# Rebuilding the preparation of an attention training kernel: token-major projections, DMA transposes, compact 16-row transposes in DRAM and zero-padded head tiles

## The chip, the cores and the metric

The kernel runs on one core of one Trainium2 chip. The metric is device time of one launch in microseconds (us), lower is better. Engines are named as the profile names them: PE (TensorE matmuls), DVE (VectorE), ACT (ScalarE), POOL (GpSimd) and SP (SyncE, which here only issues DMAs; the profile writes SPq for its sequencer).

## The reference

A transformer block with conditioned layernorms, forward and backward in one launch. Its outputs are the block's output and nine gradients.

```python
x = A_x                                     # 1 x 2048 tokens x 512, bf16
mod = (silu(c) @ w_mod).reshape(1, 6, 1, 512)
sa, ca, ga, sb, cb, gb = mod[:, 0], ..., mod[:, 5]
h = layernorm(x) * (1 + ca) + sa            # "h1" below
q, k, v = split(h @ wqkv)                   # 32 heads of width 16
p = softmax(q @ k.T * 16 ** -0.5)
x = x + ga * ((p @ v) @ wo)
h = layernorm(x) * (1 + cb) + sb
x = x + gb * (relu(h @ w1 + b1) ** 2 @ w2 + b2)     # w1: 512 x 1792
# outputs: x, and the vjp of x for grad_out with respect to
# A_x, A_wqkv, A_wo, B_w1, B_b1, B_w2, B_b2, c, w_mod
```

The kernel replaces the row maximum of the softmax by a bound: minus the norm of q times the largest norm of k of that head ("m rows"). It rides in the score matmul as a 17th row next to the 16 rows of q.

## The kernel before: what the change and the argument touch

Scores are computed for four heads at once, each in 32 rows of a 128-row tile: 16 rows of data, one auxiliary row, 15 zero rows. `n` is 2048, `P` 128, `D` 512, `TT` 16, `HG` 8 (groups of four heads, called "heads" below when the backward loads them), `QC` 4.

Preparation: layernorm, transposes on PE, token-major q/k/v, then the projections once more, now with padded weights, to get q, k and v transposed and padded:

```python
    POOL.memset(vaug[:], 1.0)
    # ... (cut) wqkv_nat loaded
    POOL.memset(wpadT[:], 0.0)
    # ... (cut) wqkv_nat copied into wpadT in slots of 32 columns; wpad_st stored
    for t in range(TT):
        ln_stats(x0_tok[:, t, :], mean1, rstd1, t, wk)      # about ten small DVE operations
        # ... (cut) xn1, h1t by DVE, h1_st stored; xn1 transposed by PE into xn1T
    # ... (cut) sum over tokens of grad_out by 16 matmuls -> gradient of b2
    for t in range(TT):
        for which in range(3):
            # 4 matmuls into pq
            if which < 2:
                DVE.tensor_copy(qtmp[:, 0:D], pq[:])
                # ... squares and sums for the norms by DVE; q_st / k_st stored
            else:
                DVE.tensor_copy(vaug[:, t, 0:H, 0:DH], pq.rearrange("p (h d) -> p h d", d=DH))
    # ... (cut) norms -> mrows, with 16 PE transposes
    for which, dstt in ((0, QtP), (1, KtP), (2, VtP)):
        for hg in range(HG):
            for qc in range(QC):
                pp = psB.tile([P, 512], F32, name="ppad", tag="pqkv")
                for ic in range(DC):
                    PE.matmul(pp[:], wpadT[:, ic, which, hg, :], h1T[:, ic, qc * 512:(qc + 1) * 512], ...)
                # DVE writes pp to stagep (plus auxsel, a 1 in the auxiliary row, for k and v)
            # for q: 4 row loads of mrows into stagep
            SP.dma_start(out=dstt[hg], in_=stagep[:])
```

Weight gradients of the dense part are summed over four chunks of tokens in DRAM, by DMAs that accumulate. Each piece passes through a `dwp` tile:

```python
                part = wk.tile([P, 512], F32, name="dwp", tag="dwp", bufs=3)
                DVE.tensor_copy(part[:, 0:w], acc[:, 0:w])
                if c == 0:
                    POOL.dma_start(out=dw_st[i][:, 0:w], in_=part[:, 0:w])
                else:
                    POOL.dma_start(out=dw_st[i][:, 0:w], in_=part[:, 0:w], accum_op=ALU.add)
```

Backward attention works through 512 units (64 for each of 8 heads). Each unit has 4 score matmuls, 4 dP matmuls, exponentials on ACT, two products `dS_u` on DVE, and one DMA transpose `dsT` issued by SP:

```python
        def load_head(hg):
            for key, src in (("q", QtP), ("k", KtP), ("v", VtP), ("do", dOtP)):
                st[key] = strm.tile([P, n], BF, name=f"i{key}", tag=f"i{key}")
                SP.dma_start(out=st[key][:], in_=src[hg])
            ACT.dma_start(out=qs[:], in_=q_st[:, :, hg * 64:(hg + 1) * 64])
        def transpose_unit(u):
            SP.dma_start(out=dqt[u // 4][:, qi], in_=bst[u][1].rearrange("p h k -> p (h k)"), transpose=True)
        load_head(0)
        for j in range(16):
            SP.dma_start(out=wT_pad[:, j, :], in_=wpad_st[:, j * P:(j + 1) * P], transpose=True)
        # ... (cut) the loop over units; load_head(hg + 1) is called early in head hg
```

## Time and profile before

The median of three runs was 3228.29 us (3228.0 to 3232.57).

The program falls into five stages. Their limits are taken from named operations in the trace: the first and last softmax exponential of the forward pass (`ET`), the first and last `dS_u` of the backward pass, and the end.

| stage | us |
|---|---|
| preparation: start to first ET | 290.0 |
| forward attention, dense chunks woven in: first to last ET | 1095.3 |
| dense tail: last ET to first dS_u | 194.4 |
| backward attention: first to last dS_u | 1464.0 |
| final gradients: to the end of the span | 181.4 |

Busy time of each engine in those stretches, kernel before. Columns: start and end, then length, then busy us of PE, PEld, DVE, ACT and POOL with the number of instructions, the granted PE clock, the DMA share (the time of the packets over the span of 16 engines, so it can pass 1: 1.14 below) and GB/s.

```profile
core 0: us, PE busy (x) PEld busy (x) DVE busy (x) ACT busy (x) POOL busy (x), PEclk, DMA share, GB/s
0.00:290.00 290.00, 175.34 (x803) 71.60 (x804) 213.76 (x451) 8.44 (x22) 33.46 (x62) 0.84 0.32 113
290.00:1385.40 1095.40, 906.09 (x5270) 245.31 (x5269) 341.58 (x627) 958.08 (x1034) 220.72 (x247) 0.77 0.47 100
1385.40:1579.80 194.40, 109.56 (x439) 43.32 (x439) 100.66 (x201) 11.77 (x18) 43.62 (x45) 0.76 0.70 154
1579.80:3043.80 1464.00, 1241.82 (x10212) 342.20 (x10208) 1190.75 (x1025) 1117.25 (x2203) 143.47 (x104) 0.84 1.14 205
3043.80:3225.20 181.40, 149.25 (x802) 64.80 (x801) 98.09 (x177) 46.27 (x94) 44.92 (x34) 0.90 0.44 124
```

In the preparation DVE is busy 214 of 290 us and PE 175, one after the other; ACT does almost nothing (8 us) and the DMA engines are idle two thirds of the time (0.32). Nothing of forward attention overlaps it. That is what the change goes for. The backward stage is the opposite: DMA share 1.14, with DVE, PE and ACT each busy more than three quarters of the time.

The costliest groups of instructions of the preparation, kernel before. Columns: line, engine, operation, output<-inputs, shapes and count; then busy us and mean ns of one; then the engine's idle time just before them, with what ended it.

```profile
L270 PE MATMUL ppad<-xn1T,wpadT 128*128 128x512 bf16 x384 | 97.9, 403 | 20.9 <-DVE stagep L273 16.2 <-DVE stagep L275 4.0 <-DVE vaug L246 0.5
L234 PE MATMUL pqkv<-wqkv_nat,xn1T 128*128 128x512 bf16 x192 | 48.1, 389 | 17.2 <-DVE vaug L246 13.4 <-DVE qtmp L239 2.0 <-DVE xn1T L217 1.8
L275 DVE TENSOR_SCALAR stagep<-ppad,auxsel 128x512 bf16<-128x512 f32 x64 | 48.0, 751 | 18.0 <-PE ppad L270 10.3 <-DMA stagep<-mrows 4.3
...
L108 DVE CAST crows<-cbf 1x512 f32<-1x512 bf16 x1 | 17.7, 17691 | 0.6 <-DMA cbf<-in_c_dram 0.6
```

The padded projections (`ppad`) cost twice what the q/k/v projections (`pqkv`) cost, for the same numbers laid out differently. The last line is an oddity: one cast of 512 numbers took 17.7 us, while POOL ran two large memsets.

### The profile page before, as it was taken

The page shows a single profiled execution, that of the slowest core. Times are in us where ns is not written, and L with a number is a line of the kernel's source. Part 1 is how long each engine was busy: PE and PEld are TensorE (multiplying, and loading weights), DVE is VectorE, ACT ScalarE, POOL GpSimd, SP SyncE. Part 2 cuts the span into 40 slices and gives each one's busy share as a digit, 9 for nine tenths or more (in the row PEclk, how much of TensorE's full clock was granted, in tenths as well). Part 3 has the DMA queues.
Part 4 walks back from the last instruction along what each step waited for, and adds up shares of the span by engine and source line. Part 5 has one row for each costly group of instructions (what it writes and reads, how often), then busy time and mean ns, then how long its engine had stood idle before and what let it go on. Part 6 is the DMA issues. An engine that isn't in the chain of part 4 may idle for free.

```text
span 3225.2 us, 47200 instructions
## 1 busy us (share of the span) xinstructions
PE 2582.1 (80%) x17521; PEld 767.2 (24%) x17521; DVE 1944.8 (60%) x2480; ACT 2141.8 (66%) x3369; POOL 486.2 (15%) x490
## 2 busy tenths in 40 slices
PE   2778998787887779655588888888888888988888
PEld 1222111222222222212122222222222222222233
DVE  8943001344443244345478787878878787878773
ACT  0004999898988789620178777877778787878632
POOL 3000000123122213322101010010101010000131
PEclk7987555798799779877679787988888787889889
DMA  4125011428247833968699999999999999999951
GB/s 157 61 88 168 28 30 42 77 86 214 67 96 142 138 82 87 167 119 178 195 203 200 212 197 214 200 213 203 205 208 198 213 196 215 196 213 196 220 152 57
DMA packets 1401343, 494.52 MB, mean 153 GB/s; under 512 B 1324168, under 2 KB 1364876, under 8 KB 1400728
## 3 DMA queue, kind: packets, MB, share of 16 engines
q1 hardware_dynamic: 1372216, 464.23, 72.2%
q0 software_dynamic: 12384, 25.17, 4.4%
q10 hardware_dynamic: 16512, 2.10, 0.5%
q8 instruction: 138, 2.26, 0.3%
q14 instruction: 93, 0.76, 0.1%
HBM read 93.93 MB, written 76.70 MB: 53 GB/s over the span
## 4 chain that ended last, share of the span: by engine, by line
PE 36%; DMA 24%; ACT 17%; DVE 11%; issue 7%; SPq 4%; POOL 1%; DVEq 0%; ACTq 0%; POOLq 0%
DMA dsT<-dS_u 16%; ACT ET L580 11%; PE psS_u L739 7%; PE dqacc L794 5%; ACT E_u L741 5%; PE accVK L776 3%; PE ppad L270 3%; PE accVK L767 2%; PE psST L578 2%; PE psS_x L739 2%; DVE dS_u L753 2%; PE pm L417 2%; PE pm L499 1%; PE pm L437 1%; PE pwq L989 1%
## 5 line engine op out<-in xcount | busy, mean ns | idle before, releaser
L753 DVE TENSOR_TENSOR dS_u<-psD_u,E_u 128x1024 bf16<-128x1024 f32 x1024 | 1188.5, 1217 | 279.3 <-PE psD_u L751 180.7
L741 ACT ACTIVATE E_u<-psS_u 128x512 bf16<-128x512 f32 x1536 | 869.3, 636 | 297.8 <-PE psD_u L751 284.2
L580 ACT ACTIVATE ET<-psST 128x1024 bf16<-128x1024 f32 x1024 | 949.8, 1260 | 136.0 <-PE psST L578 134.7
L739 PE MATMUL psS_u<-ik,iq 32*128 32x512 bf16 x1536 | 522.3, 438 | 14.0 <-DMA ik<-KtP 4.8
L751 PE MATMUL psD_u<-iv,ido 32*128 32x512 bf16 x2048 | 452.0, 435 | 36.0 <-DVE dS_u L753 30.9
L578 PE MATMUL psST<-qt_sb,kt_sb 32*128 32x512 bf16 x2048 | 399.1, 478 | 66.5 <-ACT ET L580 31.2
L741 ACT ACTIVATE E_u<-psS_x 128x512 bf16<-128x512 f32 x512 | 335.7, 656 | 23.2 <-PE psD_u L751 21.8
L794 PE MATMUL dqacc<-dsT,KS_tok 128*32 128x512 bf16 x2048 | 213.8, 505 | 165.7 <-DMA dsT<-dS_u 150.1
L594 PE MATMUL oacc<-ET,vaug 128*32 128x512 bf16 x2048 | 253.7, 486 | 1.3 <-DVE ostage L598 1.3
L776 PE MATMUL accVK<-E_u,dOs_tok 128*16 128x512 bf16 x2048 | 227.2, 434 | 1.2 <-DMA dOs_tok<-dOs_st 1.2
L739 PE MATMUL psS_x<-ik,iq 32*128 32x512 bf16 x512 | 212.3, 415 | 0.4
L809 POOL TENSOR_TENSOR dQacc<-dQacc,dqtmp 128x512 f32<-128x512 f32 x64 | 81.0, 1266 | 856.9 <-ACT dqtmp L804 856.9
L739 PEld LDWEIGHTS <-iq 32*128 32x128 bf16 x2048 | 100.0, 93 | 367.4 <-issue 366.9
L751 PEld LDWEIGHTS <-ido 32*128 32x128 bf16 x2048 | 124.3, 93 | 244.0 <-issue 218.9
L598 DVE COPY ostage<-oacc 128x512 f32<-128x512 f32 x32 | 22.0, 686 | 264.4 <-PE oacc L594 264.4
L578 PEld LDWEIGHTS <-kt_sb 32*128 32x128 bf16 x2048 | 83.8, 95 | 404.4 <-issue 393.6
L347 DVE COPY dwp<-pm 128x512 f32<-128x512 f32 (+1 forms) x102 | 67.2, 659 | 172.3 <-PE pm L340 91.3
L340 PE MATMUL pm<-tk,h_c 128*128 128x512 bf16 (+1 forms) x256 | 70.8, 408 | 70.5 <-DVE dwp L347 57.5
L767 PE MATMUL accVK<-dS_u,qz_12963 128*32 128x512 bf16 x1024 | 114.3, 435 | 7.5 <-ACT vkb L779 6.8
L767 PE MATMUL accVK<-dS_u,qz_12962 128*32 128x512 bf16 x1024 | 111.2, 424 | 7.1 <-ACT vkb L779 5.9
L270 PE MATMUL ppad<-xn1T,wpadT 128*128 128x512 bf16 x384 | 97.9, 403 | 20.9 <-DVE stagep L273 16.2
L794 PEld LDWEIGHTS <-KS_tok 128*32 128x32 bf16 x2048 | 52.4, 106 | 225.6 <-issue 170.3
(657 smaller groups left out, 2415.5 us busy)
## 6 DMA issues: line engine op xcount, KB each, us to landing
dw_st<-dwp POOLq DMA_DIRECT2D x90, 256.0 KB, 5.0
kt_sb<-KtP SPq DMA_DIRECT2D x32, 512.0 KB, 4.5
dsT<-dS_u SPq DMA_TRANSPOSE x512, 4.8
dwp<-dw_st SPq DMA_DIRECT2D x30, 256.0 KB, 5.0
wA<-in_B_w_dram SPq DMA_DIRECT2D x4, 1792.0 KB
wB<-in_B_w_dram SPq DMA_DIRECT2D x4, 1792.0 KB
QtP<-stagep SPq DMA_DIRECT2D x8, 512.0 KB, 2.9
KtP<-stagep SPq DMA_DIRECT2D x8, 512.0 KB, 2.6
```

The lines of the kernel that those rows point to most:

```text
L270: PE.matmul(pp[:], wpadT[:, ic, which, hg, :], h1T[:, ic, qc * 512:(qc + 1) * 512], start=(ic == 0), stop=(ic == DC - 1))
L578: PE.matmul(ps[:, hi, :], kt_sb[r:r + 32, kt * P:(kt + 1) * P], qt_sb[r:r + 32, :], start=True, stop=True, tile_position=(r, 0))
L580: ACT.activation(ET[:, 2 * pair:2 * pair + 2, :], ps[:], AF.Exp, scale=SCALE)
L594: PE.matmul(oacc[32 * hq:32 * hq + 32, :], lhsT, ET[:, hq, :], start=(kt == 0), stop=(kt == TT - 1), tile_position=(0, 32 * hq), skip_grou ...
L739: PE.matmul(psS[:], st["q"][r:r + 32, qt * P:(qt + 1) * P], st["k"][r:r + 32, kc * 512:kc * 512 + 512], start=True, stop=True, tile_positi ...
L741: ACT.activation(bst[u][0][:, hq, :], psS[:], AF.Exp, scale=SCALE)
L751: PE.matmul(psD[:, hi, :], st["do"][r:r + 32, qt * P:(qt + 1) * P], st["v"][r:r + 32, kc * 512:kc * 512 + 512], start=True, stop=True, til ...
L753: DVE.tensor_tensor(dS_u[:, 2 * pair:2 * pair + 2, :], psD[:], E_u[:, 2 * pair:2 * pair + 2, :], ALU.mult)
L767: PE.matmul(cur["vk"][32 * hq:32 * hq + 32, :], hst[hg]["qz"][:, qt, hq, :], bst[u][1][:, hq, :], start=(qt == 0), stop=False, tile_positi ...
L776: PE.matmul(acc[32 * hq:32 * hq + DH, :], dOs_tok[:, qt, (hg * 4 + hq) * DH:(hg * 4 + hq + 1) * DH], E_u[:, hq, :], start=False, stop=(qt ...
L794: PE.matmul(acc[32 * hq:32 * hq + 32, :], KS_tok[:, kc * 4 + kt, h * DH:h * DH + 32], tT[:, :, hq * 4 + kt, :], start=(kt == 0), stop=(kt ...
L809: POOL.tensor_tensor(dst2, dst, tmp[:], ALU.add)
```

## The change

The intent is to compute q, k and v once, token-major, to let the DMA engines transpose them, to keep the transposes compact in DRAM (16 rows for each head, no padding), and to load those rows into tiles whose padding was written once. Norms come from PE, with a selector matrix. Evictions are shared with ACT. In return every head tile is loaded in pieces of 16 rows (and one row). The padded weights for the last stage are built and transposed during forward attention instead of at the start of the backward. h1 is not stored but computed again in the last stage, and two buffers of `dwp` instead of three make room.

The core of the diff (cuts marked):

```diff
+    def load_rows(dst, srcT, hg, cols, aux=None):
+        for h in range(4):
+            i = hg * 4 + h
+            SP.dma_start(out=dst[32 * h:32 * h + DH, :], in_=srcT[i * DH:(i + 1) * DH, cols])
+            if aux is not None:
+                SP.dma_start(out=dst[32 * h + DH:32 * h + DH + 1, :], in_=aux[i:i + 1, cols])
# ... preparation (cut)
+        def layernorm(g):                    # groups of four token tiles, bn_stats/bn_aggr, xn1 by ACT
+                if ti % 2 == 1:
+                    SP.dma_start(out=h1T[:, t - 1:t + 1].rearrange(...), in_=h1_g[...], transpose=True)
+        def qkv(g):
+                for which in (1, 0, 2):      # 4 matmuls each
+                    if which == 0:
+                        DVE.tensor_copy(dst, pq[:])
+                    else:
+                        ACT.activation(dst, pq[:], AF.Identity)
+                SP.dma_start(out=qkT[:, :, t * P:(t + 1) * P], in_=qkv_g[:, ti, 0:2 * D], transpose=True)
+            SP.dma_start(out=qkT_st..., in_=qkT[:, :, cols])       # and v_st, k_st, q_st
+        def norms(g):
+            DVE.tensor_tensor(sq[:], qkT[:, :, cols], qkT[:, :, cols], ALU.mult)
+            # 8 matmuls with sel into pn[0:H]
-        for hg in range(HG):                 # the 384 padded projections, QtP, KtP, VtP (cut)
# ... forward attention (cut)
-        racc = ffw.tile([P, 4, D], F32, name="racc")
+        racc = ffw.tile([P, 5, D], F32, name="racc")   # 5th row: sum of grad_out, formerly by PE in preparation
-                part = wk.tile([P, 512], F32, name="dwp", tag="dwp", bufs=3)
+                part = wk.tile([P, 512], F32, name="dwp", tag="dwp", bufs=2)
-            SP.dma_start(out=kt_sb[:], in_=KtP[hg])
+            load_rows(kt_sb, qkT_st[1], hg, slice(0, n))
+        def later_stage(i):                  # 16 steps: v transposed, padded weights built and transposed to wT_st
# ... backward (cut)
-                SP.dma_start(out=st[key][:], in_=src[hg])
+            load_rows(hs["k"], qkT_st[1], hg, slice(0, n))
+            load_rows(hs["q"], qkT_st[0], hg, slice(0, n), m_st)
+            load_rows(hs["v"], vT_st, hg, slice(0, n))
+            load_rows(st["do"], dOT_st, hg, slice(0, n), d_st)
-        for j in range(16):
-            SP.dma_start(out=wT_pad[:, j, :], in_=wpad_st[:, j * P:(j + 1) * P], transpose=True)
+        SP.dma_start(out=wT_pad[:], in_=wT_st.rearrange("j p d -> p j d"))
# ... final stage (cut)
-        SP.dma_start(out=h1J[:], in_=h1_st[:])
+            POOL.tensor_tensor(h1J[:, t, :], xn1[:], ca1_bc, ALU.mult)
+            DVE.tensor_tensor(h1J[:, t, :], h1J[:, t, :], sa_bc, ALU.add)
```

## The prediction

> **What bounds the kernel now.** The busy table by stretches gives five stages: preparation 0 to 290 us (first exponential ET at 290.0), forward attention to 1385 (ACT busy 100% at first[...]), the dense tail to about 1580, backward attention to 3045 (512 dsT transposes, DVE dS_u at 1217 ns twice per unit; four units take about 10.5 us), final gradients to 3225. Preparation is serial to the rest. By groups of lines, PE ppad takes 97.9 us and its evictions 48.0 + 21.8 us, the q/k/v matmuls 48.1 us; one DVE CAST took 17.7 us while two POOL memsets ran[...].
>
> **What the change does to preparation.** Removed: the 384 padded projection matmuls, PE transposes, big POOL memsets, padded weights, g_b sums. Left on PE: 192 q/k/v matmuls (48 us) plus about 90 others. ACT takes two of three evictions. Added: 8 transposes of h1 and 16 of qk (256 KB each; dsT moves 512 KB in about 2.8 us), about 10 MB of stores, 6.5 MB of loads before the first h1 transpose in the same queue (the old w_mod load moved 3 MB in 10.1 us, so about 22 us). My estimate: first q/k/v matmul at 28, last at 85 to 95, then transpose, norms, m rows, store, reload: first ET at about 122 us (105 to 145). Gain 168 us, all critical.
>
> **Elsewhere.**
> - Junction to backward: by the DMA-issuing engine's timeline, 16 wT_pad transposes take 1.26 us each as backward starts (its first four units take 31.9 us, not 15), the chain 8.4 us waiting for iqs. Both move early. Gain about 25 us.
> - Backward head loads: 24 small DMAs per head replace 4 large ones and one of 2048 small pieces. Issue takes 0.5 to 0.6 us each (stagep<-mrows 0.58), so about 12 us without a dsT issue per head. But the old loads already cost about 12 us per head (first three groups of four units: 14, 14, 15 us). Net loss 0 to 20 us in all.
> - Forward: dwp has 2 buffers instead of 3, and its stores land 4 to 6 us after issue (before: 76 us of DVE idle waiting for them), so pieces come every 2.5 to 3 us instead of 1.8 to 2.6: loss about 15 us. Early weight work may delay a kt load: 5 us. Dense tail, two dwp buffers and head loads: loss about 10 us.
> - Final stage: h1 recomputed on POOL and DVE (0.42 us x16): loss 3 us.
>
> **Sum:** 3228 - 168 - 25 + 10 + 15 + 5 + 10 + 3 = about 3078; I say 3075 us, range 3030 to 3130; faster 0.96, same 0.035, slower 0.005.
>
> **What would show it.** First ET near 122 us; forward from first to last ET 1095 us before, 1105 to 1125 after; DVE dwp idle for its stores well above 76 us; first four backward units near 15 us; in each head one stretch of about 12 us without dsT issue, head period near 182 us still.
>
> **What would make it wrong.** Stores and transposes sharing DMA queues could push the first ET to 150; the row loads could stall backward by more than 8 us a head (7 heads), or the lost small-piece load could speed it up by 5 us a head; the granted PE clock (0.5 in early forward) could reach into the dense chunks.

## The result, and the profile after

The changed kernel took 3084.02 us (median of four, 3083.81 to 3086.69); the kernel before took 3230.43 us in the same rounds (3228.0 to 3236.81). The ratio is 0.9546, with a 95% interval from 0.9529 to 0.9562: faster by 4.5%. Ratios here and below are the mean time of one kernel's runs over that of the other's runs of the same rounds, so not quite the ratio of the medians that are quoted.

| stage (profiled run) | before, us | after, us | difference | predicted |
|---|---|---|---|---|
| preparation | 290.0 | 103.9 | -186.1 | -168 |
| forward attention | 1095.3 | 1119.5 | +24.2 | +15 +5 |
| dense tail to first dS_u | 194.4 | 200.0 | +5.6 | |
| backward attention | 1464.0 | 1468.1 | +4.1 | |
| tail and backward together | 1658.4 | 1668.1 | +9.7 | -25 +10 +10 |
| final stage | 181.4 | 190.7 | +9.3 | +3 |
| sum | 3225.2 | 3082.2 | -143 | -150 |

The stretches of the kernel after, in the same columns as before:

```profile
0.00:103.90 103.90, 63.23 (x286) 25.90 (x287) 53.13 (x120) 42.88 (x69) 26.98 (x30) 0.92 0.90 237
103.90:1223.40 1119.50, 907.47 (x5277) 244.73 (x5274) 331.16 (x627) 960.63 (x1033) 227.81 (x257) 0.77 0.47 98
1223.40:1423.40 200.00, 109.00 (x433) 43.51 (x433) 101.53 (x202) 11.54 (x18) 50.54 (x47) 0.78 0.67 140
1423.40:2891.40 1468.00, 1231.38 (x10212) 342.58 (x10211) 1188.10 (x1024) 1115.57 (x2204) 145.16 (x105) 0.85 1.12 200
2891.40:3082.20 190.80, 149.56 (x802) 64.67 (x801) 111.37 (x194) 46.14 (x94) 69.32 (x50) 0.90 0.38 107
```

In the first stretch PE work fell from 175 to 63 us and DVE work from 214 to 53, while ACT rose from 8 to 43 and the DMA share from 0.32 to 0.90: the work moved onto the engines that had been idle. In every later stage PE, ACT and DVE do nearly the same work as before, and yet each stage is somewhat longer. Only the last has visibly more of it on DVE (98 to 111 us) and POOL (45 to 69); POOL has 7 us more in the dense tail (44 to 51). In the backward stage the 512 transposes of 512 KB make 183 of the 200 GB/s.

The costliest groups of the preparation after:

```profile
L214 PE MATMUL pqkv<-wqkv_nat,h1T 128*128 128x512 bf16 x192 | 43.8, 384 | 7.8 <-DVE qkv_g L218 6.8 <-DMA h1T<-h_g 0.5 <-ACT qkv_g L220 0.5
L220 ACT ACTIVATE qkv_g<-pqkv 128x512 bf16<-128x512 f32 x32 | 18.9, 595 | 23.4 <-PE pqkv L214 23.4
...
L236 DVE TENSOR_TENSOR sq<-qkT 128x4096 bf16<-128x4096 bf16 x4 | 9.2, 2293 | 14.8 <-DMA qkT<-qkv_g 10.2 <-PE pqkv L214 4.6
```

`ppad` and its evictions are gone, and the 192 q/k/v matmuls now wait only 7.8 us in all. The 186 us split as follows, by the times of the first and last q/k/v matmul:

| part of preparation | before | after | difference |
|---|---|---|---|
| start to first q/k/v matmul | 88.7 | 24.5 | -64 |
| the q/k/v matmuls | 63.5 | 54.6 | -9 |
| after them, to first ET | 137.8 | 24.8 | -113 |

So the largest part is the padded projections that are no longer there. The next is that layernorm no longer stands in front of the matmuls: before, 37 to 89 us were layernorm on DVE alone (50.5 of 52 us busy); after, the first matmuls start when the first group is transposed, and the other groups overlap with them.

**Where some of it was given back.** The DVE copies into the two `dwp` buffers, first the kernel before, then after; the last part is the idle time of DVE in front of them and what ended it.

```profile
L347 DVE COPY dwp<-pm 128x512 f32<-128x512 f32 (+1 forms) x102 | 67.2, 659 | 172.3 <-PE pm L340 91.3 <-DMA dw_st<-dwp 76.4 <-PE psST L578 4.6
```

```profile
L338 DVE COPY dwp<-pm 128x512 f32<-128x512 f32 (+1 forms) x102 | 67.3, 660 | 229.7 <-DMA dw_st<-dwp 152.3 <-PE pm L331 61.2 <-PE psST L567 16.2
```

The wait for the stores doubled, from 76.4 to 152.3 us. DVE is busy only 331 of the 1119.5 us of this stage. But PE's next dense matmul waits for the copy to free its accumulator (69.9 us of such waits before, 97.6 after), and the exponentials of forward attention wait behind that on PE: ACT's waits for scores rose from 134.7 to 157.9 us, by about what the stage lost.

**The junction to the backward pass.** The chain of waits that ended last, kernel before; columns: start us, length us, what.

```profile
1569.41 8.38 DMA iqs<-q_st
...
1579.22 1.25 SPq L818
1580.51 7.85 SPq L818
...
1605.83 1.26 SPq L818
...
1607.19 4.40 DMA dsT<-dS_u
```

The same view of the kernel after, then SP's timeline there (start us, length us, engine, line, operation, output<-input, count):

```profile
1417.06 1.80 POOL iv_12083 L680
...
1426.11 2.77 POOL qz_12075 L760
1428.97 14.69 DMA dsT<-dS_u
```

```profile
1422.09 6.79 SPq L857 DMA_DIRECT2D wT_pad<-wT_st  x1
1428.97 11.36 SPq L799 DMA_TRANSPOSE dsT<-dS_u  x1
```

Before, the 8.4 us load of `iqs` and then sixteen transposes of the weights (line 818, an issue of 1.26 us in the median) stood in front of the first `dsT` transpose. After, both are gone from the chain, but POOL memsets of the freshly allocated tiles stand in it, and SP cannot issue the first `dsT` until 1428.97, because the one large load of `wT_pad` held it for 6.79 us. That transpose then takes 14.7 us, issued behind three loads of 2 MB each (`dOs_tok`, `KS_tok`, `wT_pad`). The first group of four backward units lasts 31.9 us before and 20.4 after. The prediction had said 15. The first `dS_u` itself came hardly sooner after the dense part: before, PE's first scores waited 4.8 us for the load of `ik`; after, they wait 3.4 us for a DVE copy (`prows`) that stands behind a RECIPROCAL of 3.34 us, which both kernels have.

**The head loads in the backward pass.** Each head is sixteen groups of four units, and a usual group takes about 10.5 us. Lengths of the groups, from the start times of every eighth `dS_u`:

```
                 group 1   2     3     4     5     6     7   ...  whole head
before, head 1     15.3  13.7  14.3   9.7  12.1   9.0  12.8  ...    182.3
after,  head 1     11.9  14.0  19.5  11.1   9.7  11.0  10.1  ...    184.3
before, mean of heads 1 to 6                                        181.3
after,  mean of heads 1 to 6                                        183.3
```

SP's timeline where the loads for the next head are issued, kernel before, then after:

```profile
1811.69 0.57 SPq L716 DMA_DIRECT2D ido<-dOtP  x1
1812.36 16.26 SPq L759 DMA_TRANSPOSE dsT<-dS_u  x6
```

```profile
1635.16 5.70 SPq L799 DMA_TRANSPOSE dsT<-dS_u  x2
1640.91 0.57 SPq L112 DMA_DIRECT2D ik_11035<-qkT_st  x1
...
1644.32 1.90 SPq L112 DMA_DIRECT2D iv_11036<-vT_st  x4
...
1648.73 0.28 SPq L114 DMA_DIRECT2D ido_11038<-d_st  x1
1649.11 15.25 SPq L799 DMA_TRANSPOSE dsT<-dS_u  x6
```

Before, a head load is one issue between two transposes. After, 21 of the 24 row loads go out back to back, from 1640.91 to 1649.11 (about 0.3 us each), and for those 8.2 us no transpose is issued. The third group is the one that pays (19.5 us), and the first group gains (11.9 instead of 15.3 us), which fits the old `q_st` load of 2048 small pieces being gone (16512 packets in queue q10 before, 1152 after); no run tests that alone. DVE's waits for PE in front of `dS_u` show the stall as their longest, in 1350 us of backward, before and after (us in total, times, longest):

```profile
DVE dS_u L753 <- PE psD_u L751: 163.7, 114, 4.9
```

```profile
DVE dS_u L793 <- PE psD_u L791: 192.1, 113, 10.7
```

### The profile page after: what moved, and what is told of

Its sections match the earlier page's. It is cut to its first block, busy times and chain, and to the rows that moved or that the text cites. A ratio compares the mean times of both kernels' runs of the same rounds, so it can differ in the third digit from the quotient of the medians.

```text
span 3082.2 us, 46295 instructions
## 1 busy us (share of the span) xinstructions
PE 2460.6 (80%) x17006; PEld 721.4 (23%) x17006; DVE 1785.3 (58%) x2165; ACT 2176.8 (71%) x3415; POOL 519.8 (17%) x487
## 3 DMA queue, kind: packets, MB, share of 16 engines
q10 hardware_dynamic: 1152, 2.10, 0.3%
## 4 chain that ended last, share of the span: by engine, by line
PE 32%; DMA 21%; ACT 17%; issue 11%; DVE 9%; SPq 3%; POOL 3%; DVEq 0%; POOLq 0%; ACTq 0%
DMA dsT<-dS_u 14%; ACT ET L569 12%; PE psS_u L779 7%; PE dqacc L834 5%; ACT E_u L781 5%; PE accVK L816 3%; DVE dS_u L793 3%; PE accVK L807 3%; PE psST L567 2%; PE psS_x L779 2%; PE pm L410 2%; DMA dwp<-dw_st 2%; PE pm L430 1%; PE pm L492 1%; DMA dw_st<-dwp 1%
## 5 line engine op out<-in xcount | busy, mean ns | idle before, releaser
L569 ACT ACTIVATE ET<-psST 128x1024 bf16<-128x1024 f32 x1024 | 952.3, 1249 | 158.7 <-PE psST L567 157.9
L779 PE MATMUL psS_u<-ik_11035,iq_11037 32*128 32x512 bf16 x768 | 260.2, 435 | 8.8 <-DVE prows L712 3.4
L779 PE MATMUL psS_u<-ik_12082,iq_12084 32*128 32x512 bf16 x768 | 255.0, 425 | 3.9
L791 PE MATMUL psD_u<-iv_11036,ido_11038 32*128 32x512 bf16 x1024 | 225.2, 433 | 14.1 <-DVE dS_u L793 10.8
L567 PE MATMUL psST<-qt_sb_107,kt_sb_105 32*128 32x512 bf16 x1024 | 203.4, 480 | 33.6 <-ACT ET L569 10.9
L791 PE MATMUL psD_u<-iv_12083,ido_12085 32*128 32x512 bf16 x1024 | 219.4, 422 | 6.7 <-DVE dS_u L793 3.9
L567 PE MATMUL psST<-qt_sb_108,kt_sb_106 32*128 32x512 bf16 x1024 | 195.1, 477 | 27.1 <-ACT ET L569 14.3
L338 DVE COPY dwp<-pm 128x512 f32<-128x512 f32 (+1 forms) x102 | 67.3, 660 | 229.7 <-DMA dw_st<-dwp 152.3
L779 PE MATMUL psS_x<-ik_11035,iq_11037 32*128 32x512 bf16 x256 | 106.1, 415 | 0.4
L779 PE MATMUL psS_x<-ik_12082,iq_12084 32*128 32x512 bf16 x256 | 101.9, 398 | 0.3
```

The source lines that it names most:

```text
L567: PE.matmul(ps[:, hi, :], kt_sb[r:r + 32, kt * P:(kt + 1) * P], qt_sb[r:r + 32, :], start=True, stop=True, tile_position=(r, 0))
L569: ACT.activation(ET[:, 2 * pair:2 * pair + 2, :], ps[:], AF.Exp, scale=SCALE)
L779: PE.matmul(psS[:], st["q"][r:r + 32, qt * P:(qt + 1) * P], st["k"][r:r + 32, kc * 512:kc * 512 + 512], start=True, stop=True, tile_positi ...
L791: PE.matmul(psD[:, hi, :], st["do"][r:r + 32, qt * P:(qt + 1) * P], st["v"][r:r + 32, kc * 512:kc * 512 + 512], start=True, stop=True, til ...
```

## The experiments

All twelve runs gave the reference's result. Stages with unchanged code move by a few us between profiled runs. The backward with the code of the change took 1467.5 to 1474.1 us in six kernels, with the code before 1463.4 to 1464.2 in four; the forward of the changed kernels took 1113.5 to 1120.5 us with two `dwp` buffers. So a difference of under about 7 us in one of these stages is not read from a single pair of runs. Preparation is steadier (first ET at 103.3 to 103.9 us in four kernels with the code of the change), and so is the mean of heads 1 to 6 (183.1 to 184.2 us in the six kernels, 181.0 to 181.3 in the four).

### dwp3: the third dwp buffer back

Is the forward loss the lost buffer, or something else in the stage (the row loads, the weight work done early, DVE's extra row sum)? The third buffer needs room, so the sum of grad_out goes back to PE, as a piece for each chunk, accumulated in DRAM.

```diff
-        racc = ffw.tile([P, 5, D], F32, name="racc")
+        racc = ffw.tile([P, 4, D], F32, name="racc")
-                part = wk.tile([P, 512], F32, name="dwp", tag="dwp", bufs=2)      # three places
+                part = wk.tile([P, 512], F32, name="dwp", tag="dwp", bufs=3)
+        def g_piece(c, g_c):       # replaces rowsum(4, ...): 4 matmuls, a copy, one accumulating store of a row
```

> The changed kernel with three dwp buffers again (the room comes from summing grad_out with four matmuls and one more accumulated row per chunk, instead of a fifth 2 KB row sum on POOL). Theory: the 24 us that forward attention lost (1095 to 1119 us from first to last ET) and part of the 7 us lost in the dense tail come from the third dwp buffer that was taken away; then forward falls to 1095 to 1103 us, PE idle for pm behind DVE dwp from 98 us back to about 70 us, total 3050 to 3068 us. Rival: the loss comes from the row loads and weight work on the DMA-issuing engine; then forward stays at 1115 to 1122 us and the total within 5 us of 3084.

Measured: 3057.42 us, 0.9468 [0.9437, 0.9498], against 0.9546 for the change alone. Forward attention took 1093.5 us, as before the change (1095.3), and the dense tail 192.2 (before 194.4). The same group of copies:

```profile
L338 DVE COPY dwp<-pm 128x512 f32<-128x512 f32 (+1 forms) x102 | 67.3, 660 | 198.1 <-DMA dw_st<-dwp 101.8 <-PE pm L331 84.5 <-PE psST L577 9.6
```

The whole forward loss is undone with the row loads and the early weight work still in place, though PE's waits for the copies fell only from 97.6 to 79.1 us, not to the 70 that was expected. Over all kernels that share the change's dense part, forward took 1113.5 to 1120.5 us with two buffers (six kernels) and 1093.3 to 1096.7 with three (four). It was the buffer, with whatever the moved sum of grad_out adds; this run does not part those two.

### b_dwp2: one buffer fewer in the kernel before

The mirror image: if the buffer is the cause, taking it from the kernel before should cost about the same.

```diff
-                part = wk.tile([P, 512], F32, name="dwp", tag="dwp", bufs=3)      # three places
+                part = wk.tile([P, 512], F32, name="dwp", tag="dwp", bufs=2)
```

> The kernel before with two dwp buffers and nothing else. Theory: forward grows from 1095 to 1112 to 1125 us, the dense tail from 194 by 3 to 10 us, total 3247 to 3265 us. Rival (row loads and weight work are to blame): total within 8 us of 3230.

Measured: 3272.69 us, 1.0133 [1.0101, 1.0165]. Forward attention 1136.8 us (+41), dense tail 204.6 (+10).

```profile
L347 DVE COPY dwp<-pm 128x512 f32<-128x512 f32 (+1 forms) x102 | 67.2, 659 | 228.9 <-DMA dw_st<-dwp 149.9 <-PE pm L340 74.0 <-PE psST L578 3.9
```

The wait for stores is the one seen after the change (149.9 against 152.3 us), so the buffer alone makes it. The loss in time (about 43 us in all by the ratio; the profiled run was the longest of the four) is larger than the change's own 24 us, and larger than expected. Why the kernel before suffers more from the same waits is not settled.

### spread: one row load for each unit, still on SP

If the stall in the third group comes from the loads standing in one block, spreading them should remove it.

```diff
+                spread.extend(row_list(hg))          # in load_head, in place of the 24 load_rows issues
...
+                    if pair == 0 and spread:         # in the loop over units
+                        dst, src = spread.pop(0)
+                        SP.dma_start(out=dst, in_=src)
```

> The changed kernel with the 20 row loads of the next head put one to a unit in backward, not in one block. Theory: the slow third group of each head (20.5 us against 10.5 usual) comes from about 12 us in which the DMA-issuing engine issues row loads and no dsT; then the third group falls to 11 to 14 us, the next four or five groups rise by up to 1 us each, a head falls from 183.5 to 177 to 181 us and the total to 3045 to 3070 us. Rival: the rows' traffic on the DMA engines costs the time wherever it stands; then the head stays at 182 to 185 us and the total within 8 us of 3084.

Measured: 3099.14 us, 0.9594 [0.9566, 0.9622], slower than the change itself by about 15 us. Head 1 now reads 9.6, 15.4, 12.1, 11.6, 12.5, 11.2, 12.7: the group of 19.5 us is gone, and the groups after it are all a little longer. The mean of heads 1 to 6 rose from 183.3 to 184.8 us. SP's timeline in that head:

```profile
1646.93 0.56 SPq L883 DMA_DIRECT2D ik<-qkT_st  x1
1647.60 2.29 SPq L813 DMA_TRANSPOSE dsT<-dS_u  x1
1649.93 0.77 SPq L883 DMA_DIRECT2D iq<-qkT_st  x1
```

The theory failed in the form it had: the stall can be moved, but the cost stays. In the change the issue of a `dsT` lasts 2.4 us (median of 512), so four of them fill 9.7 us of a usual group of 10.5. This includes waiting: the shortest lasted 1.32 us, and the trace does not say what the rest waits for. Between transposes a row load also lasts longer: the 24 of a head took SP 19 to 22 us here, and 9 to 10 us in one block. That left the question whether the cost is SP's time or the traffic.

### poolq: the loads of heads 1 to 7 issued by POOL

```diff
-            SP.dma_start(out=dst[32 * h:32 * h + DH, :], in_=srcT[i * DH:(i + 1) * DH, cols])
+            eng.dma_start(...)                       # eng is POOL for hg > 0, SP for hg == 0
```

> The changed kernel with the head loads of heads 1 to 7 in backward issued by POOL, same bytes, same place in the program. Theory (issue time on the one engine that also issues dsT): third group falls from 20.5 to 11 to 14 us with no cost elsewhere, head 174 to 178 us, total 3035 to 3055 us. Rival (traffic): head stays at 182 to 185 us, total within 8 us of 3084.

Measured: 3072.85 us, 0.9509 [0.9475, 0.9543], some 12 us better than the change. Heads 1 to 6 fell to 180.9 us, but a stall of 18.1 us appeared in the second group, with the DMA share at 1.20 in it and PE waiting 6.6 us in one piece for a `dsT`. Also, the first head's first group was back to 30.9 us. The expectation's "same place in the program" did not hold in time: the kernel fixes the order of PE, ACT and DVE only, and POOL issued the 24 loads for head 1 from 1429.4 to 1455.1 us, around the first `dsT` (which landed after 25.0 us instead of 14.7), while in the change SP issued 22 of them from 1451.6 us on. combo_pool below leaves head 1 to SP, and its first group takes 20.9 us. So freeing SP helped, and a block of loads from another engine still costs. The theory was half confirmed: SP's issue time, or the loads' place in SP's queue, is a part of the cost, a burst of loads is another, or the change of issuer and queue itself is (in the change q0 carries POOL's DMAs, q1 SP's), or the moment at which POOL issues; the runs do not part these.

### h1st: h1 stored and loaded again

```diff
+            SP.dma_start(out=h1_st[:, 4 * g:4 * g + 4, :], in_=h1_g[:])
...
+        SP.dma_start(out=h1J[:], in_=h1_st[:])
-            POOL.tensor_tensor(h1J[:, t, :], xn1[:], ca1_bc, ALU.mult)
-            DVE.tensor_tensor(h1J[:, t, :], h1J[:, t, :], sa_bc, ALU.add)
```

> The changed kernel, but h1 is stored in preparation (four 512 KB stores, 2 MB) and loaded in the final stage as before, not computed again on POOL and DVE. Theory 1: the final stage lost 9 us (181 to 191 us from the last dS_u on) to the second computation of h1; then it falls to 180 to 184 us. Theory 2 on preparation: PE sets its pace and the DMA engines have room; then the first ET moves from 104 by at most 3 us. Rival for preparation: the DMA engines (share 0.99 between 24 and 80 us) set the pace; then 2 MB more at 236 GB/s move the first ET by 7 to 9 us. Total 3074 to 3080 us if both theories hold.

Measured: 3077.98 us, 0.954 [0.9525, 0.9556]. The final stage took 181.4 us, exactly as before the change; the recomputation was the whole of its loss (the other edit in this stage, two buffers of `x0J` and `dx1J` instead of three, is still in). In the middle of that stage DVE is busy 74.6 of 90 us before, 87.0 of 98 after, and 75.8 of 91 here. So 12.4 us more of DVE work went with a stretch 8 us longer, and without the recomputation both are gone but for 1 us. The first ET came at 107.0 us, 3.1 us later for 2 MB more of stores. The theory that the DMA engines set preparation's pace had said 7 to 9. The net over the whole program is too small for these rounds.

### late: SP's queue freed for the first transposes

In the trace of the change SP is held 7.98 us by the issue of one small load (`cbf`) just before the first h1 transpose. Is that on the path? The edit moves it and two other loads behind the first q/k/v group, where small DVE copies (not shown) make them wait for the first transposes.

```diff
-        SP.dma_start(out=wmod_nat[:, :, 2 * D:], in_=wmod_v[:, :, 2 * D:])     # and b1bf, cbf and the silu rows
...
+            if g == 0:                                                        # after the first q/k/v group
+                SP.dma_start(out=wmod_nat[:, :, 2 * D:], in_=wmod_v[:, :, 2 * D:])
```

> The changed kernel with the loads of the last two thirds of w_mod, of b1 and of the second c held back until the first h1 transposes have landed. In the changed kernel the first h1 pair is ready at about 13.5 us but its transpose is issued at 20.1 us, after 8 us in which the DMA-issuing engine is held at the small c load behind 2 MB and 1792 two-byte pieces. Theory: the queue of loads holds the first q/k/v matmul at 24.5 us; then it starts at 18 to 20 us and the first ET at 97 to 100 us, total 3077 to 3081. Rival: other things set the pace behind it (PE or DMA engines), so the first ET stays within 2 us of 104.

Measured: 3082.53 us, 0.9552 [0.9538, 0.9566]: the same as the change. The first q/k/v matmul came 6.7 us earlier (17.8 instead of 24.5), the last only 2.7 us earlier (76.4), and the first ET at 104.3, not earlier at all. The stretch of the q/k/v matmuls, in the columns of the stage tables, first the change, then this kernel:

```profile
24.50:79.10 54.60, 47.35 (x209) 20.21 (x210) 28.97 (x49) 28.57 (x46) 12.81 (x8) 1.00 0.97 238
```

```profile
17.80:76.40 58.60, 52.11 (x212) 21.52 (x217) 36.93 (x77) 31.74 (x52) 13.51 (x8) 0.97 1.01 244
```

The DMA share is about 1 in both: the loads that were moved out of the way in front came back inside. About 13 MB pass in this stretch of the change (238 GB/s for 54.6 us), and 14.3 MB in late. Together with h1st (2 MB more, 3.1 us) this suggests that PE (47 of 55 us busy, at the full granted clock) and the DMA engines are both near their limit here; which of the two sets the pace was not tested alone.

### alldve: all evictions of q, k and v on DVE

```diff
-                    if which == 0:
+                    if which <= 2:
                         DVE.tensor_copy(dst, pq[:])
```

> The changed kernel with all 48 q/k/v evictions in preparation on DVE (0.69 us each), none on ACT. Theory: with ACT taking 32 of 48, PE sets the pace of preparation (192 matmuls in 54.6 us); with DVE alone, DVE has 29 + 22 us of work in those 56 us plus waits, so the first ET moves later by 4 to 15 us, total 3088 to 3099. Rival: the eviction engine does not matter, first ET within 2 us of 104.

Measured: the last q/k/v matmul at 82.7 us instead of 79.1, the first ET at 106.1 instead of 103.9. The whole took 3088.56 us, spread over 3079.7 to 3096.5, so the total says nothing at this size (0.957 [0.9547, 0.9592]). DVE was busy 46.8 of 56 us in the stretch, so it could still keep up. Sharing the evictions with ACT, which looks like an important part of the change, is worth about 2 us.

### b_split and b_memlate: the long CAST of the kernel before

In the trace of the kernel before the CAST of 17.7 us stands beside POOL's two memsets: they run from 1.59 to 19.44 us, it runs from 2.02 to 19.71. That it waits for the end of the memset that is running was the guess. If so, memsets cut into 28 short ones should let the CAST in between. b_split does that in the kernel before:

```diff
-    POOL.memset(vaug[:], 1.0)
+    for t in range(TT):
+        POOL.memset(vaug[:, t], 1.0)
-    POOL.memset(wpadT[:], 0.0)
+    for ic in range(DC):
+        for w in range(3):
+            POOL.memset(wpadT[:, ic, w], 0.0)
```

> The kernel before with its two long POOL memsets cut into 16 and 12 short ones. Theory: the DVE CAST of 17.7 us waits[...], and so holds the first mod matmul at 22 us; with short memsets the CAST takes under 3 us, the first mod matmul starts at 11 to 13 us (w_mod lands at 11.2) and the first ET moves from 290 to 278 to 283 us. Rival: the CAST waits for something else; then all stay within 2 us.

Measured: 3229.17 us, 1.0006 [0.9985, 1.0026]. The timeline of DVE, b_split:

```profile
2.00 18.79 DVE L108 CAST crows<-cbf 1x512 f32<-1x512 bf16 x1 [0.57 <-DMA cbf<-in_c_dram]
```

The CAST still took 18.79 us and ended at 20.8 us, just after the last memset (20.5 us). As stated, the theory was refuted: the shorter memsets did not let the CAST in, and why is not shown. Was it the memsets at all? b_memlate holds them back until the modulation columns are there, by making each wait for a value computed later:

```diff
+    POOL.tensor_copy(vaug[:, 0, 0, 0:1], modcol[:, 1, 0:1])
     POOL.memset(vaug[:], 1.0)
+    POOL.tensor_copy(wpadT[:, 0, 0, 0, 0:1], modcol[:, 1, 0:1])
     POOL.memset(wpadT[:], 0.0)
```

> The kernel before with the two POOL memsets held back until the mod columns are written (nothing else moved). After b_split failed: if the 17.7 us CAST waits for POOL's memsets, cut or whole, it now takes under 1.5 us, and the first mod matmul starts at 11 to 13 us; the first ET then moves from 290 by 3 to 12 us, less if the memsets now meet the layernorm on DVE. If the CAST waits for something else, it stays at 17 to 19 us.

Measured: 3239.64 us, 1.0016 [0.9993, 1.0039]. DVE's timeline, b_memlate:

```profile
2.03 0.41 DVE L108 CAST crows<-cbf 1x512 f32<-1x512 bf16 x1 [0.60 <-DMA cbf<-in_c_dram]
...
31.04 9.49 DVE L207 TENSOR_SCALAR xn<-x_tok,mean,rstd 128x512 bf16<-128x512 bf16 x2
```

The CAST takes 0.41 us without memsets beside it, so it did wait for them. The first modulation matmul came at 11.8 us instead of 22.3 and layernorm at 25.4 instead of 36.7, but the q/k/v matmuls still at 88.3 (88.7). The memsets now meet layernorm, and there the wait comes back: the first of the two TENSOR_SCALARs above took 8.88 us (the median of 16 is 0.41) and ended at 39.92 us, when the memset of `wpadT` did (39.77), while reductions beside the memsets took their usual 0.68 us. So the long CAST was real and had its cause in POOL's memsets, beside which the prediction had set it; how they hold it back is not shown. What it was worth stays open: b_memlate did not only take a wait of 17 us away, it brought 8.5 us back in layernorm, and a kernel without either wait was not run.

### combo_sp, combo_pool, combo_act: the parts together

combo_sp is the change with the edits of dwp3 and h1st. combo_pool adds the edit of poolq for heads 2 to 7. combo_act adds to combo_sp the edit of spread, with the loads issued by ACT:

```diff
                     if pair == 0 and spread:
                         dst, src = spread.pop(0)
-                        SP.dma_start(out=dst, in_=src)
+                        ACT.dma_start(out=dst, in_=src)
```

> The changed kernel with three dwp buffers (as dwp3) and h1 stored and loaded (as h1st). If the two gains are independent: first ET 105 to 107 us, forward 1092 to 1096 us, last ET to first dS 190 to 194 us, final stage 180 to 183 us, total 3043 to 3055 us. If they overlap or the second eats into the first, 3056 to 3065.

> combo_sp with the head loads of heads 2 to 7 in backward issued by POOL. From poolq (heads 1 to 6 there 180.9 us against 183.3): 6 heads by 2 to 3 us less, total 8 to 18 us under combo_sp. If the gain of poolq was chance, within 5 us of it.

> combo_sp with the 20 row loads of each next head spread one to a unit and issued by ACT. If the issue time on the engine that issues dsT was what spread paid for (its groups with row loads took 12 to 13 us, not 10.5), those groups fall to 10.5 to 11.5 us, a head to 176 to 180 us and the total 20 to 45 us under combo_sp. If the rows' own traffic between the dsT transposes is the cost, or ACT's time is, the heads stay at 182 to 187 us and the total is not under combo_sp.

Measured, in one set of rounds (before: 3231.75 us):

| kernel | us | ratio | forward | to first dS_u | backward | final |
|---|---|---|---|---|---|---|
| combo_sp | 3049.11 | 0.9437 [0.9418, 0.9456] | 1096.7 | 191.1 | 1468.6 | 182.6 |
| combo_pool | 3030.72 | 0.9377 [0.9359, 0.9395] | 1093.3 | 188.8 | 1459.7 | 178.6 |
| combo_act | 3011.93 | 0.932 [0.930, 0.934] | 1093.8 | 190.9 | 1437.0 | 179.7 |

The gains of dwp3 and h1st add up. Of combo_pool's 18 us only 9 are in the backward stage, where its edit is; the rest is spread over stages with unchanged code, at the size of their scatter. combo_act gains 31.6 us in the backward stage itself: heads 1 to 6 take 178.4 us, below the kernel before (181.3). Its backward stage, in the columns of the stage tables, and the longest wait in 1350 us of it:

```profile
1391.30:2828.30 1437.00, 1239.29 (x10212) 339.67 (x10211) 1192.33 (x1024) 1118.23 (x2204) 146.21 (x107) 0.84 1.16 204
```

```profile
DVE dS_u L819 <- PE psD_u L817: 148.2, 119, 4.7
```

The engines do the same work in less time, and the wait of 10.7 us is gone. The same spreading on SP gained nothing (spread), so spreading alone is not the reason; taking the loads off SP is. That changed two things at once. The 24 loads of a head took SP 19 to 22 us in spread and take ACT 7 us here (median 0.31 us each). And they go through another DMA queue: in the backward stage queue q10, which carries what ACT issues, moved 1.84 MB in spread and 9.41 MB here, while SP's transposes stay in q1. Whether the cost was SP's time or the place in SP's queue, no run parts. Whether a whole block issued by ACT would do as well was not run, so the share of the spreading within combo_act stays open. combo_act is the best version found, 2.3% under the change (0.932 against 0.9546).

It is the row loads that move to ACT; all transposes stay on SP in every kernel here.

## Why the prediction was right or wrong

The total was right (3075 predicted, 3084 measured, inside 3030 to 3130), and so was the reason: preparation was serial to the rest, and its gain is nearly the whole gain. Term by term:

- **Preparation, "first ET at about 122 us", gain 168.** Mechanism right, size too small: 103.9, gain 186, just outside the stated 105 to 145. The start (28 predicted, 24.5 measured) was about right. The last q/k/v matmul was put at 85 to 95 and came at 79.1, and what follows it was put at 27 to 37 us and took 24.8. Both terms allowed for the transposes and stores slowing PE. The DMA engines were indeed full (share 0.97), but PE still ran 47 of 55 us, waiting 7.8 us. The feared 150 did not come; in late and alldve, freeing SP's queue in front or burdening DVE moved the first ET by 0.4 and 2.2 us only.
- **The CAST of 17.7 us.** The cause was shown (b_memlate: 0.41 us without the memsets beside it). Its worth in the kernel before was not: the q/k/v matmuls began at 88 to 89 us with and without it, but in b_memlate the wait had moved into layernorm. The sum did not count it on its own.
- **Junction, "gain about 25 us".** Mis-sized: the first group of four units fell by 11.5 us (31.9 to 20.4), and the way from the last dense matmul to the first `dS_u` by 1.5 (8.5 to 7.0), 13 in all. Two steps failed. "First four backward units near 15 us" took the sixteen weight transposes away and put nothing in their place; the trace shows one issue holding SP for 6.79 us and three loads of 2 MB in front of the first `dsT`. And the 8.4 us for `iqs` were counted in full, where the way to the first `dS_u` shortened by 1.5: a DVE copy behind a RECIPROCAL of 3.34 us is now what PE waits for.
- **Forward, "loss about 15 us" plus "a kt load: 5 us".** 24 us measured. dwp3 gives it all to the buffer, together with the moved sum of grad_out, and b_dwp2 shows that the buffer alone costs time. The term for the kt load was zero: the first quarter of the stage, which has no dense work, took 233.9 us before and 234.0 after. So 15 should have been about 24.
- **Dense tail and head loads, "about 10 us", and "net loss 0 to 20 us".** The tail up to the last dense matmul lost 7.1 us and heads 1 to 7 about 14 (2 each). The mechanism of the head loads was as described, one stretch without a `dsT` issue in each head, of 8.2 us instead of about 12. The period, "near 182 us still", was 183.3. Together that is 21 against 20 in the sum, where the 0 to 20 of the text stood as 10; how the 21 divide between the `dwp` buffers and the head loads was not parted.
- **Final stage, "loss 3 us".** 9.3 measured, and h1st shows that it is all the recomputation. The term counted the 0.42 us of a DVE operation on part of the tiles as if the rest would hide on POOL. DVE was already busy 83% (74.6 of 90), the 16 added operations took 0.48 us each there, and POOL took 1.5 us for each of its own.

The total came out as close as it did partly by luck, because the errors cancelled: preparation gave 18 us more than predicted, while the junction (12), forward (4), the final stage (6) and the small rest took away about 25.

## What to carry to other kernels

When a serial stage runs on one engine while others idle, moving layout work to the DMA engines can pay (290 to 104 us here, with the padded projections gone); but look afterwards at each stage with unchanged work, because what made room (a buffer fewer, a value computed again) was charged there: 24 and 9 us here, both recoverable. Look at the sequencer that issues DMAs, and at its queue, as at an engine with a budget: where it is held 2.4 us for each transpose of a 2.6 us period, even loads of 0.3 us were better on another issuer and its queue (combo_act, 31.6 us less in the backward), and spreading them on the same one did not help. The issues of the change were no constant: plain ones took, for example, 0.28 us (a row of 4 KB), 6.79 us (`wT_pad`, 2 MB) and 7.98 us (`cbf`, a row of 1 KB behind the large first loads; what held it was not tested). A large wait in a profile is only worth what the next limit leaves of it: the queue hold of 8 us was removed, and the time did not move. And a wait that an edit takes away in one place can come back in another, as the CAST of 18 us did; look for it before calling it worthless.
